# An attention layer and two feed-forward layers on one core: the sums of resident weights go from GpSimd to VectorE, and one block's gate goes to ScalarE

## The chip, the cores and the metric

The kernel runs on one core of a Trainium2 chip, as one program. The time is the device time in microseconds (us), and less is better. A run's time is the median of several executions; the profile is of one execution. The engines are TensorE (PE; its weight loads are PEld), VectorE (DVE), ScalarE (ACT), GpSimd (POOL), and SyncE (SP), which here only issues DMAs.

## The reference

The input is q, k, v of shape (4, 8, 576, 64), a memory matrix and norm for each head, a gate beta, and the weights of two feed-forward layers with 512 model columns and 2048 hidden columns. All is float32.

```
scores = softmax(causal(q k^T / 8));  local = scores v
mem    = (phi(q) M_prev) / (phi(q) z_prev),  phi(x) = max(x,0) + exp(min(x,0))
x      = g * mem + (1 - g) * local, g = sigmoid(beta)     -> 2304 tokens x 512
h1     = x w_in1;  y  = (s * relu(h1)^2 + b) w_out1       first layer
h2     = y w_in2;  out = (h2 * tanh(softplus(h2))) w_out2 second layer
```

## The kernel before, in words

**Precision.** TensorE multiplies float32 matrices as two halves: a high part rounded by a copy (`h`) and a low part, the difference (`l`). Each product is three matmuls: high by high, high by low, low by high. ACT makes the high part of a matrix, DVE the low one (`split`, lines 724 and 725, and the like elsewhere).

**Tokens.** The first layer runs 1024 tokens in four small blocks of 256, then one big block of 512 (`first` and `y_part`, lines 860 and 939). Its last 768 tokens, and all 2304 of the second layer in three times 768, go through a seven-product scheme for 2x2 blocks (`hidden` and `out_product`, lines 1094 and 1167 or 1170). That scheme does not use the weights themselves but sums and differences of their quarters.

**Weights of the first layer.** They are converted early and stay in SBUF, in four parts `r`, as high and low parts (`wih`, `wil`, `woh`, `wol`). For the seven products their sums have to be made from both parts again: 16 tables of nine additions of 128x256 elements each, 144 in all. `resident` (line 787) does this, for the input weights by `IN_TABLE` and for the output weights by `OUT_TABLE`; line 794 is the addition. Four results of each table are stored to DRAM (line 804) and loaded again later, when the seven products want them. All of it is on POOL (`E_SUMS = 'PP'`). The ring `c1` holds the intermediate values in four buffers of 256 columns; they lie in `stage` columns that the first conversion uses before (`conversion_left`). A table takes seven of these buffers, one for each name on its left side, and a stored one comes free when the store has landed.

**Weights of the second layer.** They are converted after the attention has ended (`convert`, lines 687 to 704, and `combine_in`, `combine_out`, whose sums are line 739 and whose splits are line 725). DVE does two steps on each of 32 pieces (lines 701 and 703), and the sums. Two of its work buffers, and the five split buffers `sp`, come to be when the small blocks have left their space (`small_left`).

**The gate of the first layer**, s * relu(h)^2 + b. For a small block, pairs of 256 columns at a time: ACT scales h by s (line 911), DVE multiplies by max(h, 0) (line 917), ACT adds b and rounds to the high part (line 920), DVE makes the low part (line 922). For the big block ACT does it all but the low part: relu (911), square (914), affine (915), high part (919); DVE makes the low part (921). PE's next product into the bank has to wait until the gate has read it.

**The order.** Each operation is a step with an engine, an assumed duration and a key. `Plan.order` simulates all engines ahead of time: whenever an engine is free it takes the ready step with the smallest key, and so it fixes the order of each engine's instructions in the program, SP's too. Engines then run their own instructions strictly in that order. Keys: gates and other elementwise work of the first layer -1 (negative ones first), attention 0 to below 220, first-layer products 500 and up, sums of resident weights and the copies of the weights 499 (`COMBINE`), second conversion 655.2 (`CONV2`), loads and the seven products 990 and up. The plan knows nothing of two engines that slow each other down.

Of the kernel before, what the change touches and what calls it, by code (L numbers as in the profile page):

```python
# [19 lines left out]
P = 128  # L20
# [15 lines left out]
E_SUMS = 'PP'  # L36
# [25 lines left out]
def pool2_us(n):  # L62
    return 0.08 + 0.0028 * n

# [110 lines left out]
class Step:  # L175
    def __init__(self, engine, us, prio, f, waits, bufs, new):
        self.engine, self.us, self.prio, self.f = engine, us, prio, f
        self.waits, self.bufs, self.new = waits, bufs, new
        self.next, self.next_start, self.opens, self.ready = [], [], [], 0.0
        self.lag, self.mode = 0.0, 0  # L180


class Plan:
# [53 lines left out]
    def order(self):  # L237
# [20 lines left out]
        while True:  # L258
            e = 0
            while e < 6:  # L260
# [39 lines left out]
                else:  # L300
                    got.done = end + got.lag
                busy[e] = True
# [43 lines left out]
def attention_then_two_ffn(ctx: ExitStack, tc: tile.TileContext, qk, qz, vm, beta,  # L346
# [108 lines left out]
    def pair(b, p, prio, g, place=None, apart=False):  # L455
# [4 lines left out]
        def add(engine, us, f, r=(), w=(), keep=(), share=1.0):  # L460
            attention_steps.append(plan.add(engine, us, prio, f, r, w, keep=keep, share=share))

# [59 lines left out]
        add(DVE, dve_us(n_e), lambda: nc.vector.scalar_tensor_tensor(ex.t, q_rows(), 0.0, ex.t, op0=ALU.max, op1=ALU.add), [ex, qn_b], [ex])  # L522
        add(DVE, dve_us(n_e), lambda: nc.vector.tensor_tensor(q_rows(), ex.t, z().to_broadcast([P, 2, n_t, D]), op=ALU.mult), [ex, qn_b], [qn_b])
# [149 lines left out]
    def convert(layer, prio, which, r, j, raw, after=()):  # L673
# [10 lines left out]
        def f32():  # L684
# [16 lines left out]
        add(DVE, 0.6, prio, lambda: nc.vector.scalar_tensor_tensor(words()[:, :, 0], words()[:, :, 1], -2 ** 31, words()[:, :, 0],  # L701
                                                                   op0=ALU.bitwise_and, op1=ALU.bitwise_or), [raw, low_words], [signed])
        add(DVE, 0.6, prio, lambda: nc.vector.scalar_tensor_tensor(w.t, w.t, 3, words()[:, :, 0], op0=ALU.logical_shift_left,  # L703
                                                                   op1=ALU.bitwise_or), [raw, signed, w], [w])
# [13 lines left out]
    def split(prio, t, src, r, after=(), done=()):  # L718
# [6 lines left out]
        lo = add(DVE, dve_us(n), prio, lambda: nc.vector.tensor_tensor(t[0](1), src(), t[0](0).bitcast(F32), op=ALU.subtract),  # L725
                 [*r, half], [t[2]], after)
# [8 lines left out]
    def sums(prio, out, table):  # L735
        for f in table:
# [4 lines left out]
            add(DVE, dve_us(256), prio, one, out[1:], out[:1])  # L741
# [45 lines left out]
    def resident(e, prio, hi, lo, names, shape, table, bufs, landed, dest):  # L787
# [4 lines left out]
        def one(o_, x, y, op):  # L792
            def f():
                (nc.vector if e == DVE else nc.gpsimd).tensor_tensor(view(made[o_].t, shape, F32), *(view(made[k].t, shape, F32) if k in made else (hi, lo)[k[0] == "l"](k[1:])
                                                                        for k in (x, y)), op=op)

            steps.append(add(e, dve_us(256) if e == DVE else pool2_us(256), prio, f, [*bufs, *(made[k] for k in {x, y} if k in made)], [made[o_]]))

        for o_, x, y, op in table:
            if o_ not in made:  # L800
                made[o_] = Buf(R["c1"], [P, 256])
            one(o_, x, y, op)
            if o_ in names and (o_, x, y, op) == [row for row in table if row[0] == o_][-1]:
                steps.append(add(DMA, load_us(256), prio, lambda o_=o_: nc.sync.dma_start(dest(names.index(o_)), view(made[o_].t, shape, F32)),
                                 [made[o_]], [landed]))
                steps[-1].lag = 1.5
        return steps

    IN_TABLE = (("A00", "h00", "l00", ALU.add), ("A11", "h11", "l11", ALU.add), ("S1", "h10", "A11", ALU.add), ("S1", "S1", "l10", ALU.add),
                ("S0", "S1", "A00", ALU.subtract), ("S2", "A00", "h10", ALU.subtract), ("S2", "S2", "l10", ALU.subtract),  # L810
                ("A01", "h01", "l01", ALU.add), ("S3", "A01", "S0", ALU.subtract))
# [608 lines left out]
```

## Time and profile before

| | |
|---|---|
| median of three runs | 978.67 us (976.68 to 979.77) |
| the profiled execution | 978.76 us, span 977.0 us |
| PE busy | 944.4 us, 97% |
| PEld busy | 865.5 us, 89% |
| DVE busy | 799.1 us, 82% |
| ACT busy | 666.0 us, 68% |
| POOL busy | 312.5 us, 32% |
| granted TensorE clock, mean | 0.995 |

The span is the time from the first to the last instruction. A busy time is the sum of an engine's instructions with overlaps taken out; matmuls are pipelined, so that a busy PE may still run below its peak. The stages in time: attention with small blocks beside it, and the first conversion, up to about 345 us; small blocks and then the big one, with the second conversion, up to about 505 us; then the seven products of the first layer's rest and of the second layer. In lists of waits, the idle time of an engine before an instruction is put down to what came last of the things the instruction waited for.

### The profile page before, as it was taken

Reading aid. Unit: us, or ns where it says so; the run is one execution under the profiler, and the core shown is the slowest. Engines: PE = TensorE matmul, PEld = TensorE weight load, DVE = VectorE, ACT = ScalarE, POOL = GpSimd, SP = SyncE. Lnnn points to the kernel's source line nnn. Section 1 sums busy time; section 2 is a strip of 40 time slices with the busy share of each in tenths; the row PEclk is TensorE's granted clock in tenths of the full one; section 3 lists DMA queues with packets and bytes.
Section 4 is the critical chain, followed back from the end, with each engine's and each line's share of the span. In section 5 each row is a group of like instructions: output and inputs, shape, how many; then the busy total and the mean of one; then the engine's idle time right before and its main releaser. Section 6 shows DMA issues by size and latency. Waiting matters only on the chain.

```text
span 977.0 us, 19335 instructions
## 1 busy us (share of the span) xinstructions
PE 944.4 (97%) x6599; PEld 865.5 (89%) x6599; DVE 799.1 (82%) x1782; ACT 666.0 (68%) x1433; POOL 312.5 (32%) x495
## 2 busy tenths in 40 slices
PE   5899899999999999998999999999999999999998
PEld 5668688787787899886899999999999999999998
DVE  5999999777767389999887899799966799677874
ACT  4889888877877655668989986467643566344652
POOL 5542566776776756871000000000010000100000
PEclk9999999999999999999999999999999999999999
DMA  9864846999995379899998735896587656676444
GB/s 237 260 192 125 271 143 200 249 273 258 283 268 151 95 215 278 269 301 309 315 336 288 235 124 188 317 335 224 172 297 229 225 173 195 223 235 210 159 144 174
DMA packets 148563, 224.11 MB, mean 229 GB/s; under 512 B 15344, under 2 KB 122864, under 8 KB 141552
## 3 DMA queue, kind: packets, MB, share of 16 engines
q1 hardware_dynamic: 141408, 174.63, 57.9%
q0 software_dynamic: 6624, 48.24, 14.7%
q8 instruction: 52, 0.85, 0.4%
q14 instruction: 47, 0.39, 0.1%
q10 hardware_dynamic: 432, 0.01, 0.0%
HBM read 159.39 MB, written 63.44 MB: 228 GB/s over the span
## 4 chain that ended last, share of the span: by engine, by line
PE 45%; issue 7%; DVE 6%; ACT 6%; DMA 5%; POOL 1%; SPq 0%; POOLq 0%; DVEq 0%; ACTq 0%
PE bank L1094 18%; PE bank L1167 13%; PE bank L1170 6%; PE bank L939 3%; PE bank L860 3%; DMA wo_sums_d<-stage 1%; DVE sc L739 1%; DVE stage L701 1%; DMA woh<-wi_split_d 1%; DMA wi_d<-sc 1%; DVE w32b L703 1%; PE bank L637 1%; DMA woh<-x_d 1%; DVE gl L922 1%; PE bank L615 1%
## 5 line engine op out<-in xcount | busy, mean ns | idle before, releaser
L1094 PE MATMUL bank<-wi,woh 128*128 128x384 f32 x546 | 118.5, 336 | 1.3 <-ACT wol L1112 0.6
L1167 PE MATMUL bank<-wol,S 128*128 128x256 f32 x792 | 107.3, 283 | 0.0
L1167 PEld LDWEIGHTS bank<-wol,S 128*128 128x128 f32 x792 | 101.0, 192 | 0.0
L1094 PEld LDWEIGHTS bank<-wi,woh 128*128 128x128 f32 x546 | 96.2, 188 | 3.2 <-ACT wol L1112 0.9
L1167 PE MATMUL bank<-woh,S 128*128 128x256 f32 x720 | 97.4, 283 | 0.0
L1094 PE MATMUL bank<-wi,wol 128*128 128x384 f32 x414 | 96.1, 335 | 0.0
L1167 PEld LDWEIGHTS bank<-woh,S 128*128 128x128 f32 x720 | 91.4, 192 | 0.0
L574 ACT ACTIVATE Pt<-Pt,mx 128x64 f32<-128x64 f32 (+4 forms) x152 | 83.0, 569 | 3.2 <-DVE mx L566 3.2
L620 ACT COPY PT<-bank 128x384 f32<-128x384 f32 (+2 forms) x160 | 68.8, 492 | 22.8 <-PE bank L615 19.8
L1094 PEld LDWEIGHTS bank<-wi,wol 128*128 128x128 f32 x414 | 73.9, 188 | 0.9 <-DVE woh L1100 0.6
L577 POOL TENSOR_SCALAR Pt<-ex,nm 128x64 f32<-128x64 f32 x152 | 56.9, 396 | 51.0 <-DVE nm L526 38.2
L615 PE MATMUL bank<-ident,Pt 128*128 128x128 f32 x444 | 63.8, 280 | 8.2 <-DVE Pt L592 6.0
L566 DVE CUSTOM_DVE_ANT_0 Pt<-bank,mask 128x64 f32<-128x64 f32 (+3 forms) x152 | 52.0, 373 | 16.1 <-PE bank L556 15.5
L615 PEld LDWEIGHTS bank<-ident,Pt 128*128 128x128 f32 x444 | 51.3, 143 | 12.4 <-POOL ex L520 3.9
L1074 POOL DMA_DIRECT2D woh<-wo_split_d x13 | 6.9, 528 | 164.1 <-DVE g L1100 76.2
L860 PE MATMUL bank<-xh,wi 128*128 128x256 f32 x256 | 42.4, 294 | 5.5 <-DVE rt L917 3.3
L1068 POOL DMA_DIRECT2D woh<-wo_resident_d x4 | 2.4, 590 | 141.0 <-PE bank L1094 105.2
L725 DVE TENSOR_TENSOR woh<-stage,woh 128x1024 fp32r<-128x1024 f32 (+2 forms) x38 | 39.0, 1027 | 9.6 <-ACT woh L724 9.5
L724 ACT CAST woh<-stage 128x1024 fp32r<-128x1024 f32 (+2 forms) x38 | 33.8, 889 | 18.4 <-PE bank L1094 15.6
L724 ACT CAST S<-g 128x384 fp32r<-128x384 f32 x56 | 28.8, 513 | 24.6 <-PE bank L1167 19.2
L917 DVE SCALAR_TENSOR_TENSOR rt<-bank,rt 128x512 f32<-128x512 f32 x32 | 22.0, 686 | 24.8 <-ACT rt L911 24.7
L592 POOL TENSOR_SCALAR Pt<-Pt,rs 128x64 f32<-128x64 f32 (+2 forms) x72 | 38.6, 557 | 10.4 <-DVE rs L595 6.5
(317 smaller groups left out, 2695.5 us busy)
## 6 DMA issues: line engine op xcount, KB each, us to landing
woh<-wo_split_d POOLq DMA_DIRECT2D x13, 1024.0 KB, 5.2
wol<-wo_split_d POOLq DMA_DIRECT2D x11, 1024.0 KB, 5.1
stage<-in_w_in SPq DMA_DIRECT2D x21, 512.0 KB, 5.1
wol<-wi_split_d POOLq DMA_DIRECT2D x10, 1024.0 KB, 5.2
stage<-in_w_out SPq DMA_DIRECT2D x19, 512.0 KB, 5.2
stage<-wi_d SPq DMA_DIRECT2D x24, 384.0 KB, 4.8
stage<-wo_d SPq DMA_DIRECT2D x18, 512.0 KB, 3.5
wo_split_d<-high SPq DMA_DIRECT2D x32, 256.0 KB, 4.7
```

What stands on the lines that cost most here:

```text
L566: nc.vector.tensor_tensor_reduce(at_t(i, t, D + lo, D + hi), x.t[:, a:a + hi - lo], mask[:, SP - w + lo:SP - w + hi], -SCALE, mx.t[:, i, t ...
L574: nc.scalar.activation(at_t(i, t, D, w + D), at_t(i, t, D, w + D), AF.Exp, bias=mx.t[:, i, t + k:t + k + 1], scale=-1.0, accum_out=rs.t[:, ...
L577: add(POOL, 0.33, lambda i=i, t=t: nc.gpsimd.tensor_scalar(at_t(i, t, 0, D), ex.t[:, i, t - lo_t, :], nm.t[:, i, t - lo_t:t - lo_t + 1], 1 ...
L592: (nc.vector if e == DVE else nc.gpsimd).tensor_scalar(x, x, r, *((None, ALU.mult) if e == DVE else (1.0, ALU.mult, ALU.mult)))
L615: nc.tensor.transpose(ps.t[:, x, :], at_t(i, t, c * P, (c + 1) * P), ident)
L620: (nc.vector.tensor_copy if dve else nc.scalar.copy)(PT[i].t[:, x:x + n], ps.t[:, :n])
L724: hi = add(ACT, act_us(n), prio, lambda: nc.scalar.copy(t[0](0), src()), r, [t[2], half], after)
L725: lo = add(DVE, dve_us(n), prio, lambda: nc.vector.tensor_tensor(t[0](1), src(), t[0](0).bitcast(F32), op=ALU.subtract), [*r, half], [t[2] ...
L860: nc.tensor.matmul(ph, w_at(nm, r, cc)[:, o:o + P], x_at(x, cc), start=(begin and part == 0 and cc == 0), stop=(part == 2 and cc == NCC - ...
L1094: nc.tensor.matmul(ps.t[:, :H2], w[i // 4].t[:, j, kk, at_], x[kk].t[:, k], start=begin and part == kk == 0, stop=part == 2 and kk == 1, s ...
L1167: nc.tensor.matmul(acc[t].t[:, :DH], s.t[:, j, t * P:(t + 1) * P], x.t[:, k, q % 4], start=q == part == 0, stop=q == NQ2 - 1 and part == 2)
L1170: nc.tensor.matmul(acc[t].t[:, :H2], x.t[:, k, q % 4, t * P:(t + 1) * P], s.t[:, j], start=q == part == 0, stop=q == NQ2 - 1 and part == 2)
```

## The change

All 144 sums go to DVE (`E_SUMS = 'DD'`). A table now reuses a buffer where an operand is not wanted again and is not itself a result, so that it takes four buffers instead of seven; its additions are chained in the order of the table, and `IN_TABLE` is put in another order. `c1` has a fifth buffer, in the space of the small blocks, which is there from the beginning; for that reason `small_left` now also waits for all sums (`combined`). The assumed lag of a stored sum's landing is 3.0 us instead of 1.5 (`LAND`). The block `j = 3`, the fourth small one, has its gate made as the big block's (`GATED`). Steps with two inputs in SBUF are marked (`two`), and the planner adds 0.35 us (`LOCK`) to a marked step that ends its wait for the engine while a marked step runs on the other of DVE and POOL. The key of the copies of weights gets a name of its own (`KEEP`) and keeps its value.

```diff
-E_SUMS = 'PP'
+E_SUMS = 'DD'
+LOCK = 0.35
+LAND = 3.0
+KEEP = 499.0
+GATED = (3,)
...
+def two(s):
+    s.two = True
+    return s
...
+        beside = [0.0] * 6
...
                 else:
+                    if got.two and beside[DVE + POOL - e] > now:
+                        end += LOCK
                     got.done = end + got.lag
+                    beside[e] = end if got.two else 0.0
...
-        def one(o_, x, y, op):
+        def one(o_, x, y, op, after):
+            o_b, x_b, y_b = (made.get(k) for k in (o_, x, y))
             def f():
...
+            s = two(add(e, 0.05 + dve_us(256) if e == DVE else pool2_us(256), prio, f, [*bufs, *(b for b in (x_b, y_b) if b)], [o_b], after))
+            steps.append(s)
+            return s
+        done = []
         for o_, x, y, op in table:
             if o_ not in made:
-                made[o_] = Buf(R["c1"], [P, 256])
-            one(o_, x, y, op)
+                same = next((k for k in (x, y) if k in made and not any(k in row[1:3] for row in table[table.index((o_, x, y, op)) + 1:]) and k not in names), None)
+                made[o_] = made[same] if same else Buf(R["c1"], [P, 256])
+            done = [one(o_, x, y, op, done)]
...
-                steps[-1].lag = 1.5
+                steps[-1].lag = LAND
...
+    IN_TABLE = (("A11", "h11", "l11", ALU.add), ("S1", "h10", "A11", ALU.add), ("S1", "S1", "l10", ALU.add),
+                ("A00", "h00", "l00", ALU.add), ("S2", "A00", "h10", ALU.subtract), ("S2", "S2", "l10", ALU.subtract),
+                ("S0", "S1", "A00", ALU.subtract), ("A01", "h01", "l01", ALU.add), ("S3", "A01", "S0", ALU.subtract))
...
+        on_act = big or j in GATED
         add(ACT, act_us(m) - 0.04, ew, lambda: nc.scalar.activation(
-            rt.t, ph.t[:, :m], *((AF.Relu,) if big else (AF.Copy, 0.0, sb[:, 0:1]))), [ph], [rt])
-        if big:
+            rt.t, ph.t[:, :m], *((AF.Relu,) if on_act else (AF.Copy, 0.0, sb[:, 0:1]))), [ph], [rt])
+        if on_act:
+            add(ACT, act_us(m), ew, lambda: nc.scalar.activation(rt.t, rt.t, AF.Square), [rt], [rt])
+            add(ACT, act_us(m), ew, lambda: nc.scalar.activation(rt.t, rt.t, AF.Identity, sb[:, 1:2], sb[:, 0:1]), [rt], [rt])
...
-    R["c1"] = Ring("c1").homes(stage, [2048 + 256 * i for i in range(4)], conversion_left)
+    R["c1"] = Ring("c1").homes(stage, [2048 + 256 * i for i in range(4)], conversion_left).more(m1s)
...
-                small_left = add(NONE, 0.0, 0.0, close_small, after=small_steps)
+                small_left = add(NONE, 0.0, 0.0, close_small, after=[*small_steps, combined])
```

The marks stand on the low parts (lines 522 and 523 of the attention, 701, 703, 725, 739, 883, 921 and 922) and on the sums.

## Rows read from the trace of the kernel before

**Rows 1.** Windows by stage: us, each engine's busy us, PE clock, DMA share, GB/s.
```profile
75.00:182.00 107.00, 102.55 (x816) 85.12 (x816) 99.25 (x268) 91.12 (x226) 60.55 (x95) 0.98 0.66 194
182.00:350.00 168.00, 166.84 (x1369) 137.93 (x1369) 110.61 (x361) 126.86 (x343) 120.10 (x216) 1.00 0.78 225
350.00:400.00 50.00, 47.95 (x387) 47.13 (x386) 49.37 (x63) 24.36 (x40) 36.43 (x37) 1.00 0.83 253
400.00:450.00 50.00, 46.22 (x228) 38.65 (x227) 47.58 (x62) 35.16 (x63) 33.35 (x36) 1.00 0.89 278
450.00:525.00 75.00, 74.00 (x359) 64.29 (x358) 63.48 (x133) 69.31 (x137) 0.00 (x0) 1.00 1.00 332
525.00:575.00 50.00, 49.15 (x278) 47.74 (x277) 43.92 (x87) 48.99 (x94) 2.36 (x4) 1.00 0.59 194
```

**Rows 2.** TensorE's timeline: start, us, instructions, [idle before, what ended it].
```profile
364.30 1.22 PE L860 MATMUL bank<-xh,wi 128*128 128x256 f32 x8 [2.05 <-DVE rt L917]
402.29 1.20 PE L860 MATMUL bank<-yh,wi 128*128 128x512 f32 x4 [1.87 <-DVE rt L917]
442.69 1.20 PE L860 MATMUL bank<-yh,wih 128*128 128x512 f32 x4 [1.91 <-ACT g L911]
460.43 1.20 PE L860 MATMUL bank<-yh,wih 128*128 128x512 f32 x4 [0.90 <-ACT g L911]
```

**Rows 3.** ScalarE's timeline, the row ahead of the third wait.
```profile
440.11 0.41 ACT L724 CAST high<-w32b 128x256 fp32r<-128x256 f32 x1 [3.90 <-DVE w32b L703]
```

**Rows 4.** Line L794 in two windows: us, POOL busy us, clock, DMA.
```profile
182.00:350.00 168.00, 55.63 (x72) 1.00 0.78 225
350.00:450.00 100.00, 69.78 (x72) 1.00 0.86 266
```

**Rows 5.** VectorE by line, 350 to 450 us: busy us, mean ns.
```profile
L701 DVE SCALAR_TENSOR_TENSOR stage<-stage 128x512 int32<-128x512 int32 x15 | 15.1, 1008 | 0.0
L922 DVE SCALAR_TENSOR_TENSOR gl<-rt,sb,gh 128x512 fp32r<-128x512 f32 x9 | 10.5, 1172 | 0.3 <-ACT gh L920 0.3
L739 DVE TENSOR_TENSOR sc<-w32b,sc 128x256 f32<-128x256 f32 x12 | 8.0, 668 | 0.1
L917 DVE SCALAR_TENSOR_TENSOR rt<-bank,rt 128x512 f32<-128x512 f32 x9 | 6.1, 682 | 0.8 <-ACT rt L911 0.8
```

**Rows 6.** VectorE by line, 450 to 525 us.
```profile
L701 DVE SCALAR_TENSOR_TENSOR stage<-stage 128x512 int32<-128x512 int32 x7 | 4.8, 689 | 1.5 <-ACT stage L699 1.5
L739 DVE TENSOR_TENSOR sc<-w32b,sc 128x256 f32<-128x256 f32 x6 | 2.5, 422 | 0.1
```

**Rows 7.** VectorE's timeline, one L922 while POOL stands idle.
```profile
344.81 0.75 DVE L922 SCALAR_TENSOR_TENSOR gl<-rt,sb,gh 128x512 fp32r<-128x512 f32 x1 [0.19 <-ACT gh L920]
```

**Rows 8.** Line L794: ns min/median/max, first and last start; what it waited for.
```profile
L794 POOL TENSOR_TENSOR stage<-stage x32: 721/779/1177, 187.6 to 445.6; 128x256 f32<-128x256 f32 x32
...
  DMA wo_sums_d<-stage: 20.4, 14
  DMA wi_sums_d<-stage: 12.8, 4
```

**Rows 9.** VectorE's timeline, two L739 back to back.
```profile
443.62 0.41 DVE L739 TENSOR_TENSOR sc<-w32b,w32b 128x256 f32<-128x256 f32 x1
443.95 0.41 DVE L739 TENSOR_TENSOR sc<-w32b,sc 128x256 f32<-128x256 f32 x1
```

**Rows 10.** VectorE by line, 75 to 182 us.
```profile
L701 DVE SCALAR_TENSOR_TENSOR stage<-stage 128x512 int32<-128x512 int32 x12 | 9.0, 747 | 0.0
```

**Rows 11.** TensorE's waits, 75 to 182 us: total, times, longest.
```profile
PE bank L860 <- DVE rt L917: 1.2, 1, 1.2
```

**Rows 12.** ScalarE by line, whole span: square and affine steps.
```profile
L914 ACT ACTIVATE g<-g 128x512 f32<-128x512 f32 x16 | 10.1, 632 | 0.3
L915 ACT ACTIVATE g<-g,sb 128x512 f32<-128x512 f32 x16 | 13.0, 815 | 0.2
```

**Rows 13.** TensorE's timeline, the last product of the small blocks.
```profile
420.15 0.63 PE L939 MATMUL bank<-gl,woh 128*128 128x256 f32 x4
```

More of the change, by code (lines that the diff above doesn't have):

```diff
@@ L179, in __init__ @@
         self.next, self.next_start, self.opens, self.ready = [], [], [], 0.0
-        self.lag, self.mode = 0.0, 0
+        self.lag, self.mode, self.two = 0.0, 0, False
 class Plan:
@@ L461, in add @@
             attention_steps.append(plan.add(engine, us, prio, f, r, w, keep=keep, share=share))
+            return attention_steps[-1]
         n_t, lo_t, last = len(g), g[0], g[-1]
@@ L700, in convert @@
                                                           TRUNC, 2.0 ** -29 * (1.0 - 2.0 ** -16)), [raw], [low_words])
[L701 to L704, printed above, removed]
+        two(add(DVE, 0.6, prio, lambda: nc.vector.scalar_tensor_tensor(words()[:, :, 0], words()[:, :, 1], -2 ** 31, words()[:, :, 0],
+                                                                       op0=ALU.bitwise_and, op1=ALU.bitwise_or), [raw, low_words], [signed]))
+        two(add(DVE, 0.6, prio, lambda: nc.vector.scalar_tensor_tensor(w.t, w.t, 3, words()[:, :, 0], op0=ALU.logical_shift_left,
+                                                                       op1=ALU.bitwise_or), [raw, signed, w], [w]))
         if layer == 1:
@@ L724, in split @@
         hi = add(ACT, act_us(n), prio, lambda: nc.scalar.copy(t[0](0), src()), r, [t[2], half], after)
-        lo = add(DVE, dve_us(n), prio, lambda: nc.vector.tensor_tensor(t[0](1), src(), t[0](0).bitcast(F32), op=ALU.subtract),
-                 [*r, half], [t[2]], after)
+        lo = two(add(DVE, dve_us(n), prio, lambda: nc.vector.tensor_tensor(t[0](1), src(), t[0](0).bitcast(F32), op=ALU.subtract),
+                     [*r, half], [t[2]], after))
         return hi, lo
@@ L739, in one @@
                 nc.vector.tensor_tensor(o_, x, y, op=op)
-            add(DVE, dve_us(256), prio, one, out[1:], out[:1])
+            two(add(DVE, dve_us(256), prio, one, out[1:], out[:1]))
     def combine_in(prio, r, kk, w0, w1):
@@ L790, in resident @@
         made, steps = {}, []
-        def one(o_, x, y, op):
+        def one(o_, x, y, op, after):
+            o_b, x_b, y_b = (made.get(k) for k in (o_, x, y))
             def f():
-                (nc.vector if e == DVE else nc.gpsimd).tensor_tensor(view(made[o_].t, shape, F32), *(view(made[k].t, shape, F32) if k in made else (hi, lo)[k[0] == "l"](k[1:])
-                                                                        for k in (x, y)), op=op)
-            steps.append(add(e, dve_us(256) if e == DVE else pool2_us(256), prio, f, [*bufs, *(made[k] for k in {x, y} if k in made)], [made[o_]]))
+                (nc.vector if e == DVE else nc.gpsimd).tensor_tensor(
+                    view(o_b.t, shape, F32), *(view(b.t, shape, F32) if b else (hi, lo)[k[0] == "l"](k[1:]) for k, b in ((x, x_b), (y, y_b))), op=op)
+            s = two(add(e, 0.05 + dve_us(256) if e == DVE else pool2_us(256), prio, f, [*bufs, *(b for b in (x_b, y_b) if b)], [o_b], after))
+            steps.append(s)
+            return s
@@ L799, in resident @@
+        done = []
         for o_, x, y, op in table:
             if o_ not in made:
-                made[o_] = Buf(R["c1"], [P, 256])
-            one(o_, x, y, op)
+                same = next((k for k in (x, y) if k in made and not any(k in row[1:3] for row in table[table.index((o_, x, y, op)) + 1:]) and k not in names), None)
+                made[o_] = made[same] if same else Buf(R["c1"], [P, 256])
+            done = [one(o_, x, y, op, done)]
             if o_ in names and (o_, x, y, op) == [row for row in table if row[0] == o_][-1]:
-                steps.append(add(DMA, load_us(256), prio, lambda o_=o_: nc.sync.dma_start(dest(names.index(o_)), view(made[o_].t, shape, F32)),
+                steps.append(add(DMA, load_us(256), prio, lambda o_=o_, b=made[o_]: nc.sync.dma_start(dest(names.index(o_)), view(b.t, shape, F32)),
@@ L1250, in attention_then_two_ffn @@
         for which in ("in", "out"):
-            c1_steps[which][r] += keep_resident(COMBINE, which, r)
+            c1_steps[which][r] += keep_resident(KEEP, which, r)
         for kk in range(2):
```

21 lines of the change are left out of this document (8 added, 13 removed).

## The prediction

> **What bounds the kernel now.** I read the busy time by stage first, then who TensorE waited for, then the timelines around each wait. The stages [rows 1] show TensorE (PE) busy all but 1.16 us of 182 to 350 us, but short by 2.05 us in 350:400, 3.78 in 400:450, 1.00 in 450:525 and 0.85 in 525:575: 7.7 us in all. A busy PE is not PE at its peak, yet the rest of the span is matmuls that the change does not touch, so these few microseconds are what can be won. The long waits stand in [rows 2]: two of 2.05 and 1.87 us ended by VectorE's (DVE) gate L917, then 1.91 and 0.90 us ended by ScalarE's (ACT) L911. In the first two DVE was late: it is busy 49.37 of 50 us in 350:400 [rows 1]. The third is DVE's too, one step back: ACT stood 3.90 us on a split that needed DVE's L703 [rows 3], with the gate queued behind it. So one cause, a full DVE in 350 to 450 us, made 5.83 of the 7.7 us.
>
> DVE is full there partly because of GpSimd (POOL). POOL makes 72 of its 144 sums (L794) in 182:350 and 72 in 350:450, 125.4 us in all [rows 4]; meanwhile DVE's instructions with two SBUF inputs stretch: L701 takes 1008 ns, L922 1172, L739 668 in 350:450 [rows 5], against 689 and 422 ns for L701 and L739 once POOL is quiet [rows 6] and 0.75 us for L922 [rows 7]. L917, with one input in PSUM, stays at 682 ns.
>
> **The change, part by part.**
>
> *Sums leave POOL.* What DVE gets back in 350:450: 15 x (1008 - 689) = 4.8 us on L701's first form, 9 x (1172 - 750) = 3.8 on L922, 12 x (668 - 422) = 3.0 on one form of L739. These are three of some fifteen groups; the others, done alike (L703, the remaining L701 and L739, L725, L883, L921), bring the total to about 32 us of DVE's 97. In 182:350 the same relief is small, about 4 us (L922 and L883), an estimate. POOL also stood 20.4 + 12.8 us on landings of its own stores [rows 8]; that goes too.
>
> *Sums come to DVE.* No row shows a sum of this form on DVE. The nearest is L739, which has the same 128x256 f32 shape: recorded at 422 ns, but issued every 0.33 to 0.34 us back to back [rows 9]. So 144 sums cost 144 x 0.335 = 48 us by the pitch and 144 x 0.422 = 61 us by the record; I take 50, near the pitch, because a record overlaps its successor. They still share time with POOL's attention work: in 75:182 POOL was busy 60.55 us of 107, 57% [rows 1], and L701 took 747 ns [rows 10], 58 above its quiet time. With the sums gone POOL is left with 120.1 - 55.6 = 64.5 us of 168 in 182:350 [rows 1, 4], 38%; 58 x 38/57 x 144 = 5.6 us more. So some 55 us. The bounds are 48 and 61 + 5.6 = 67.
> By the Trainium skill, SBUF — State Buffer, "Who interferes with whom", a two-input Vector instruction and a GpSimd one that reads SBUF exclude each other for the whole instruction. That alone would price each sum at a share of a whole POOL instruction, and the sums here nearer the upper end; the small stretch of L701 [rows 10] says that it rarely falls so.
>
> *Where they land.* The planner gives sums key 499, behind attention (below 220) and the gates (-1), ahead of the second layer's conversion (655.2). So DVE makes them in the holes of attention, from 182 us when the stage columns come free. DVE is busy 110.6 us of 168 there [rows 1]: 57 us of holes plus 4 of relief, for 55 us of sums. Nearly all of them fit, the last by some 350 to 380 us instead of 446 [rows 8]. Five buffers in place allow that: a table now holds four buffers instead of seven. The fifth buffer is free from the start but lets only the first table's first few sums through. The planner's new lock term charges nothing: it delays a step only while the other engine runs a marked one, and with both letters D POOL has no marked step.
>
> *What this costs PE.* DVE would stand at about (110.6 + 55 - 4)/168 = 96% in 182:350. Behind a sum stand the attention's minima, the gates and the low parts, which PE's transposes and products need. Nothing shows PE's loss for this exactly. The nearest row is 75:182, the same mixture with DVE at 99.25 of 107 us [rows 1]: PE waited 1.2 us for the gate [rows 11], so 1.2 x 168/107 = 1.9 us. From above: 400:450, DVE at 95%, with the 1.87 + 1.91 us of [rows 2] traced to DVE, so 3.78 x 168/50 = 12.7 us. From below zero, since first-layer products fill attention's holes on PE. I take 2, as 75:182 is the nearer kind of work. SP's queue carries each store behind its sum, with attention's loads behind it; a late sum holds them, and that is in the same bounds.
>
> *The fourth small block's gate.* Its 8 L917 leave DVE (8 x 0.682 = 5.5 us, [rows 5]). ACT gets 8 squares and 8 affine steps, 8 x (0.632 + 0.815) = 11.6 us [rows 12], less about 2 on cheaper forms of the first and last pass. That lies beside 24.4 us of ACT's 50 in 350:400 [rows 1]; if it ran in 450:525 instead, where ACT has 69.3 of 75, it would cost its length. DVE's two late gates in [rows 2] are this block's, so both waits lose their immediate cause. DVE in 350:450 then holds 97 - 32 - 5.5 = 59 us of 100, plus whatever sums are left over, so the ACT wait of 1.91 us should go too. What is late next is DMA (332 GB/s, share 1.00 in 450:525) and ACT; both bound the second conversion, not PE directly.
>
> *Released later.* The last split buffers now wait for all sums as well as the small blocks. The small blocks' last product starts at 420 us [rows 13]; with the sums done by 380 this costs nothing.
>
> *Sum.* Against the profiled execution, 978.76 us (span 977.0; the median shown, 978.67, is the same to 0.1): -2.05 - 1.87 - 1.91 + 2 = -3.8. Of the other 1.75 us (0.90 in [rows 2] and 0.85 in 525:575) I take 1.0, because the conversion ends earlier and ACT with it (bounds 0 and 1.75): -4.8, **974.0 us**.
>
> **Rivals.**
> 1. *DVE becomes the bound of attention* (slower). If the planned holes are not there on the chip, each sum in front of a minimum or a gate moves PE. At the price of 400:450 that is 12.7 - 6.7 = +6.0, or 984.8 us. It decides once the sums need more than the 61 us of holes, which the upper bound of 67 exceeds. For it: DVE at 96% by my own count. Against: sums have the last key, and 72 of them at most overflow into a stage with 40 us to spare. By the Trainium skill, Perfetto Trace Analysis, "Optimizing Scalar/DVE Operations", a saturated Vector engine is one to take work from, even to GpSimd; the change does the reverse, and by that rule the time would be this rival's. The same section warns that these two engines share a read port, so moving work between them may not help, and the stretched rows here [rows 5, 6] put the warning first.
> 2. *Relief without time* (same). The gates' waits go (3.9), ACT's waits stay or grow because ACT has 10 us more, and attention gives 2 back: 976.9 us. For it: ACT is at 49 of 50 us in 525:575. Against: in 350:450 it idles 40 us.
> 3. *Everything goes* (faster still). All 7.7 us, and the 1.16 us of 182:350 as the plan meets durations it assumed: 969.9 us. For it: the planner's costs know no stretched DVE instruction, so without POOL the order fits better. Against: 93 to 96% of DVE in attention.
> 4. *The sums stay late*: the planner packs attention so that most sums still run after 350 us and the split buffers open late. DVE then has 59 + 50 of 100 us and nothing changes but the engine: 979 us, for the same 350:450 waits. Against: 57 us of holes.
>
> **How the numbers follow.** Chances: the forecast 0.50, rival 1 0.16, rival 2 0.14, rival 3 0.16, rival 4 0.04. A measurement of this kernel tells about 0.3% (2.9 us) from no change, so faster begins below 975.8 and slower above 981.6. The forecast's own range is 971 to 977 (waits in attention 0 to 4), of which 0.42 lies under 975.8 and 0.08 within. With rival 3 that makes 0.58 faster; 0.08 + 0.14 + 0.03 = 0.25 the same; 0.16 and a little of rival 4 make 0.17 slower. The range 967 to 981.5 takes in rivals 2, 3 and 4, with 3 us for what rival 3 may find elsewhere, and leaves out most of rival 1.
>
> **What would show it.** POOL empty of L794, and the sums as DVE rows of about 0.42 us ending before 380 us. L701 at 0.69 us and L922 at 0.75 in 350:450, DVE there near 60 to 75 us of 100. No PE wait on L917 after 350 us; L914 and L915 with 24 instances instead of 16. PE short by under 3 us in 350:575 and by 2 to 4 in 182:350. It is wrong if PE waits on DVE in 182:350 for over 6 us, if the last sum runs after 420 us, or if PE's shortfall in 350:575 stays above 5 us with DVE free.

## The result, and the profile after

The changed kernel takes 970.84 us (median of 4 runs, 969.38 to 971.16) against 979.22 for the kernel before beside it: a ratio of 0.9916 [0.9894, 0.9937], faster by some 8 us. The profiled execution took 969.38 us, its span 967.5. The line numbers moved: L701, L739, L794, L860, L911, L917 and L922 of before are L716, L754, L811, L881, L933, L939 and L944 now, and L703 is L718; where the gate is on ScalarE its low part is L943.

First the busy time by stage, to be held against [rows 1] (columns as there).

```profile
75.00:182.00 107.00, 101.69 (x798) 84.17 (x798) 102.12 (x271) 88.58 (x218) 56.58 (x88) 0.97 0.63 186
182.00:350.00 168.00, 168.00 (x1387) 139.96 (x1387) 140.98 (x462) 129.29 (x348) 77.00 (x151) 1.00 0.84 241
350.00:400.00 50.00, 50.00 (x399) 49.08 (x398) 43.14 (x97) 36.05 (x61) 0.00 (x0) 1.00 0.92 281
400.00:450.00 50.00, 50.00 (x241) 42.04 (x240) 40.49 (x83) 42.74 (x82) 0.00 (x0) 1.00 0.85 282
450.00:525.00 75.00, 74.87 (x376) 67.31 (x375) 61.37 (x126) 67.81 (x130) 0.00 (x0) 1.00 0.95 317
525.00:575.00 50.00, 48.78 (x277) 47.69 (x277) 44.04 (x85) 46.02 (x86) 2.32 (x4) 1.00 0.56 183
```

PE has no hole left from 182 to 450 us, where it was short by 1.16, 2.05 and 3.78 us. POOL is empty after 350. DVE fell from 97 to 84 of 100 us in 350:450 although it now makes sums there, and does 180 instructions instead of 125. What PE still waits for in 350:575, in place of the 6.7 us of [rows 2], is this (us in total, times, longest):

```profile
PE bank L1116 <- ACT wol L1134: 0.7, 1, 0.7
PE bank L1116 <- ACT g L1134: 0.5, 1, 0.5
```

The sums, DVE's busy us by window, against POOL's 55.63 and 69.78 of [rows 4]:

```profile
182.00:350.00 168.00, 40.35 (x97) 1.00 0.84 241
350.00:450.00 100.00, 16.37 (x41) 1.00 0.89 282
```

And DVE's instructions by line in 350 to 450 us, against [rows 5]:

```profile
L716 DVE SCALAR_TENSOR_TENSOR stage<-stage 128x512 int32<-128x512 int32 x14 | 9.6, 689 | 2.8 <-ACT stage L714 2.8
...
L754 DVE TENSOR_TENSOR sc<-w32b,sc 128x256 f32<-128x256 f32 x12 | 5.0, 420 | 0.1
...
L811 DVE TENSOR_TENSOR stage<-woh,wol 128x256 f32<-128x256 f32 x10 | 4.1, 420 | 0.0
...
L944 DVE SCALAR_TENSOR_TENSOR gl<-rt,sb,gh 128x512 fp32r<-128x512 f32 x1 | 0.7, 747 | 0.0
```

L701 went from 1008 to 689 ns, L739 from 668 to 420, L922 from 1172 to 747: the quiet values of [rows 6, 7].

The view that says most in the least space is the chain of work that ended last, cut to 345 to 480 us: shares of that window by engine and line. Before:

```profile
by line: issue 10.1%; PE bank L860 9.2%; DMA wo_sums_d<-stage 8.9%; PE bank L939 8.0%; DVE sc L739 7.0%; DVE stage L701 7.0%; DMA wi_d<-sc 6.1%; DVE w32b L703 5.3%; DMA woh<-x_d 4.8%; DVE gl L922 4.5%; DMA raw<-in_w_in 3.1%; POOL stage L794
```

After:

```profile
by line: PE bank L881 50.6%; PE bank L961 48.9%; PE bank L1116 0.4%; PE bank L957 0.3%
```

Before, the chain ran through DVE's decoding (L701, L703, L739, L922), through the landings of POOL's stores of its sums, and for 17.2% through PE's two lines. After, it is PE alone.

By milestones of the two traces, all of them starts of matmuls: the last attention product starts at 334.2 us instead of 336.4 (-2.2; below, the attention is called over at this point), the first of the seven products at 479.5 instead of 488.0 (-8.5), the outer products (L1170, now L1192) at 549.0 instead of 558.0 (-9.0), and the last product at 963.7 instead of 973.2 (-9.5). So 2.2 us come from the attention, 6.3 from 345 to 480 us, 1.0 from behind it.

### The profile page after: what moved, and what is told of

It reads as the page before. It is cut to its first block, busy times and chain, and to the rows that moved or that the text cites. A ratio compares the mean times of both kernels' runs of the same rounds, so it can differ in the third digit from the quotient of the medians.

```text
span 967.5 us, 19325 instructions
## 1 busy us (share of the span) xinstructions
PE 941.8 (97%) x6599; PEld 865.6 (89%) x6599; DVE 809.2 (84%) x1918; ACT 675.3 (70%) x1449; POOL 195.7 (20%) x351
## 4 chain that ended last, share of the span: by engine, by line
PE 85%; ACT 5%; DVE 4%; DMA 2%; POOL 1%; issue 1%; SPq 0%; POOLq 0%; DVEq 0%; ACTq 0%
PE bank L1116 20%; PE bank L1189 19%; PE bank L881 14%; PE bank L961 13%; PE bank L1192 6%; PE bank L652 5%; PE bank L630 4%; PE bank L571 4%; DMA wil<-in_w_in 1%; DVE Pt L581 1%; DMA wih<-in_qz 1%; ACT Pt L589 1%; POOL stage L710 1%; POOL Pt L592 0%; DVE stage L716 0%
## 5 line engine op out<-in xcount | busy, mean ns | idle before, releaser
L592 POOL TENSOR_SCALAR Pt<-ex,nm 128x64 f32<-128x64 f32 x152 | 60.2, 418 | 75.5 <-DVE nm L541 50.4
L881 PE MATMUL bank<-xh,wi 128*128 128x256 f32 x256 | 43.3, 299 | 4.4 <-ACT xh L903 2.9
L739 ACT CAST woh<-stage 128x1024 fp32r<-128x1024 f32 (+2 forms) x38 | 33.8, 889 | 18.6 <-PE bank L1116 15.6
L607 POOL TENSOR_SCALAR Pt<-Pt,rs 128x64 f32<-128x64 f32 (+2 forms) x72 | 43.0, 617 | 18.5 <-DVE rs L610 7.6
L739 ACT CAST S<-g 128x384 fp32r<-128x384 f32 x56 | 28.8, 514 | 24.6 <-PE bank L1189 19.2
L961 PE MATMUL bank<-gl,woh 128*128 128x256 f32 x256 | 41.8, 288 | 0.0
L881 PEld LDWEIGHTS bank<-xh,wi 128*128 128x128 f32 x256 | 36.0, 199 | 6.1 <-ACT xh L903 3.4
```

What stands on the lines that cost most here:

```text
L592: add(POOL, 0.33, lambda i=i, t=t: nc.gpsimd.tensor_scalar(at_t(i, t, 0, D), ex.t[:, i, t - lo_t, :], nm.t[:, i, t - lo_t:t - lo_t + 1], 1 ...
L881: nc.tensor.matmul(ph, w_at(nm, r, cc)[:, o:o + P], x_at(x, cc), start=(begin and part == 0 and cc == 0), stop=(part == 2 and cc == NCC - ...
L961: nc.tensor.matmul(acc[ec // per].t[:, (ec % per) * n:(ec % per + 1) * n], w_at(nm, fc // FPR, fc % FPR)[:, ec * P:(ec + 1) * P], t(x)[:, ...
```

## The experiments

All times are medians of runs beside the kernel before, whose median was 977.4 to 979.5 us in the five sets (one for the changed kernel, then e1 to e4, e5 to e8, e9 to e11, e12). Where kernels of different sets are compared, I give the difference of the times and that of the ratios, times 978.6 us.

| kernel | us | ratio to before | interval |
|---|---|---|---|
| the changed kernel | 970.84 | 0.9916 | 0.9894 to 0.9937 |
| e9: before, sums on VectorE | 967.18 | 0.9890 | 0.9871 to 0.9910 |
| e1: before, gate on ScalarE | 978.40 | 0.9994 | 0.9982 to 1.0005 |
| e12: both | 968.04 | 0.9886 | 0.9870 to 0.9902 |
| e2: changed, gate back | 976.30 | 0.9976 | 0.9963 to 0.9988 |
| e3: changed, sums back on GpSimd | 983.99 | 1.0053 | 1.0038 to 1.0069 |
| e4: changed, old buffers | 967.34 | 0.9883 | 0.9865 to 0.9900 |
| e7: e4, gate back | 970.65 | 0.9914 | 0.9899 to 0.9930 |
| e8: e4, but in place | 967.34 | 0.9881 | 0.9865 to 0.9898 |
| e10: changed, early sums held | 967.26 | 0.9894 | 0.9869 to 0.9918 |
| e11: e8, third gate moved too | 970.16 | 0.9919 | 0.9902 to 0.9936 |
| e5: changed, idle additions on GpSimd | 1011.55 | 1.0329 | 1.0310 to 1.0349 |
| e6: changed, idle memsets on GpSimd | 969.86 | 0.9902 | 0.9885 to 0.9919 |

My theory at this point was that DVE, slowed by POOL, had held back PE in 350 to 450 us, and that sums and gate each take a part of that away. The rivals were that the gate alone does it, that the sums would be as well on POOL in the new order, and that five buffers in place make it possible.

**The gate alone.**

```diff
+GATED = (3,)
...
+        on_act = big or j in GATED
         add(ACT, ... lambda: nc.scalar.activation(
-            rt.t, ph.t[:, :m], *((AF.Relu,) if big else (AF.Copy, 0.0, sb[:, 0:1]))), [ph], [rt])
-        if big:
+            rt.t, ph.t[:, :m], *((AF.Relu,) if on_act else (AF.Copy, 0.0, sb[:, 0:1]))), [ph], [rt])
+        if on_act:
...
```

> The kernel before with only the fourth small block's gate moved to ScalarE; the sums stay on GpSimd with four buffers. Theory (GpSimd's sums stretch VectorE, and the move of the sums makes most of the gain): VectorE loses 5.5 us of 97 in 350 to 450 us but its L922 and the conversion stay stretched (over 900 ns for the conversion's steps); the two waits of PE on L917 go, ScalarE's stay: 975 to 977.5 us against 979. Rival (the gate was the late thing, the sums matter little): 973 us or less.

Measured 978.40, no gain; neither said so. The stretch stayed, as the theory had it (the conversion's L703, here L704, takes 1000 ns in 345:450, the gate's low part L923 1159). Its waits of PE, 345 to 575 us:

```profile
PE bank L861 <- ACT g L913: 3.5, 2, 3.0
PE bank L861 <- ACT rt L913: 1.3, 1, 1.3
...
PE bank L937 <- DVE xr L974: 0.7, 1, 0.7
```

The two waits on DVE's gate [rows 2] are gone, and 4.8 us stand on ScalarE's step L913 (L911 of before) where 2.81 stood. The gate was where the delay showed, not what made it.

**The changed kernel without the gate's move.**

```diff
-GATED = (3,)
+GATED = ()
```

> The changed kernel without the gate's move: the sums on VectorE in place with five buffers, the fourth small block's gate on VectorE again. Theory: the stretch is gone, VectorE has 84 + 5.5 = 89 of 100 us in 350 to 450 us, PE waits there for under 2.5 us: 971 to 974 us. Rival (the gate made the gain): 975 to 978 us, with PE waiting for the multiply of the gate on VectorE.

Measured 976.30: the rival's time, but not its place. PE is busy all of 345 to 450 us without the move, so no wait on a gate came back. The loss lies behind it, as two windows of this kernel show (columns as in [rows 1]):

```profile
345.00:450.00 105.00, 105.00 (x682) 96.23 (x681) 87.62 (x182) 71.11 (x125) 0.00 (x0) 1.00 0.82 263
450.00:575.00 125.00, 120.35 (x617) 108.59 (x616) 103.74 (x211) 112.58 (x215) 2.31 (x4) 1.00 0.81 268
```

PE's longest waits in the second:

```profile
PE bank L1116 <- ACT woh L1134: 1.2, 1, 1.2
PE bank L1116 <- DVE g L1122: 1.1, 2, 0.6
PE bank L1116 <- ACT g L1134: 1.0, 1, 1.0
```

617 matmuls against 652 in the changed kernel there. These are waits for evacuations of the seven products, with the outer products at 555.5 us instead of 549.0. The plan had found another order for this stage; what in that order makes the waits I did not take apart.

**The sums back on POOL, all else kept.**

```diff
-E_SUMS = 'DD'
+E_SUMS = 'PP'
```

> The changed kernel with the sums back on GpSimd, all else kept: in place, five buffers, the gate on ScalarE, and now with the planner's lock term at work. Theory (which engine adds is what counts): the conversion's steps on VectorE stretch to over 850 ns again wherever sums run beside them; 974 to 977.5 us. Rival (fewer buffers a table and so earlier sums made the gain): 972 us or less, with the last sum before 390 us.

Measured 983.99, slower than before, so both expected times fell. The theory's stretch came (L716 881 ns, L718 983 in 345:450), the rival's early sums did not (the last one starts at 432.1 us). Yet the stretch did not hold PE back there: the lock term has something to charge in this kernel, and in the order that the plan then finds PE is only 0.46 us short in 345:450 though POOL adds there for 65 us. What is lost stands elsewhere: the attention is over at 339.6 us instead of 334.2, and behind 480 us stand longer waits and a stretch at a lower clock (columns of [rows 1]). Whether the stretch costs PE time thus depends on the order too.

```profile
345.00:450.00 105.00, 104.54 (x685) 95.79 (x684) 90.61 (x118) 75.73 (x132) 65.32 (x68) 1.00 0.85 265
450.00:525.00 75.00, 70.81 (x334) 61.83 (x333) 61.62 (x133) 64.84 (x128) 0.00 (x0) 0.95 0.96 322
510.00:520.00 10.00, 6.03 (x21) 5.02 (x20) 8.29 (x18) 6.31 (x13) 0.00 (x0) 0.66 1.00 323
```

**Buffers and order.** One buffer for each name of a table, four of them, and the small blocks' closing without its new wait:

```diff
-                made[o_] = made[same] if same else Buf(R["c1"], [P, 256])
+                made[o_] = Buf(R["c1"], [P, 256])
...
-    R["c1"] = Ring("c1").homes(stage, [...], conversion_left).more(m1s)
+    R["c1"] = Ring("c1").homes(stage, [...], conversion_left)
...
-                small_left = add(..., after=[*small_steps, combined])
+                small_left = add(..., after=small_steps)
```

> The changed kernel with one buffer for each name of a table, four slots, and the split buffers opened without the sums, as before; sums on VectorE and the gate on ScalarE. Theory: the sums end later (seven buffers a table in four slots; the last one after 400 us) but nothing on VectorE is stretched: 971 to 974 us. Rival (five buffers in place are needed for the gain, as VectorE would stand in order behind a landing): 976 us or more.

Measured 967.34: better than the changed kernel by 3.5 us (3.2 by the ratios), though the last sum starts at 421.4 us. Neither the buffers nor early sums are what pays. Nor do sums and stores that come late hold PE back by themselves: here a table takes seven buffers again, as before (last sum at 445.6), and yet PE is busy all of 345 to 450 us. The next has the last two hunks alone, so that the sums are in place in four buffers:

```diff
-    R["c1"] = Ring("c1").homes(stage, [...], conversion_left).more(m1s)
+    R["c1"] = Ring("c1").homes(stage, [...], conversion_left)
...
-                small_left = add(..., after=[*small_steps, combined])
+                small_left = add(..., after=small_steps)
```

> The changed kernel with its sums in place, but four buffers in the stage alone, and without the new wait of the small blocks' closing (the fifth buffer lies in what that closing gives back, so the two go together). It parts what cost the changed kernel some 3 us against the run with the old buffers: the sums in place, or the fifth buffer and its wait. Theory (the fifth buffer's wait and the early sums that it lets into the attention cost it): 966.5 to 968.5, the first sum after 170 us. Rival (a sum in place has to wait for the one before it on the same engine, and that costs): 969.5 to 972, with the last sum before 400 us.

Measured 967.34 again: in place or not is the same, and the theory holds. In the same set the control e6 (below), the changed kernel in all but memsets on POOL, had 969.86. The third kernel keeps the five buffers and their wait, and holds the early sums back:

```diff
-        done = []
+        done = [conversion_left]
```

> The changed kernel with one edit: the first sum of each table also waits until the first layer's conversion has left the stage, so that the fifth buffer stays but no sum runs before that (the changed kernel makes 7 before 182 us). It asks why five buffers cost 3.5 us against four. Theory (the early sums, in the attention, cost it): 966.5 to 968.5, the end of the attention at most 333 us. Rival (the fifth buffer costs it by what it lies in, or by the order that it brings later): 969.5 to 972.

Measured 967.26, 3.6 us under the changed kernel (2.2 by the ratios; the two intervals overlap, the runs themselves lie apart), attention over at 332.0 us: the theory holds. The other traces bear it out: where the early sums run (the changed kernel, e2, e5, e6) the attention is over at 334.2 to 335.7 us, and where they do not (e4, e7 to e10, e12) at 329.9 to 332.2. What the hunk holds back is three sums. DVE's timeline of the changed kernel (start, us):

```profile
105.61 0.66 DVE L811 TENSOR_TENSOR c<-wi 128x256 f32<-128x256 f32 x1
106.30 0.76 DVE L811 TENSOR_TENSOR c<-wi,c 128x256 f32<-128x256 f32 x1
107.10 0.76 DVE L811 TENSOR_TENSOR c<-c,wi 128x256 f32<-128x256 f32 x1
...
179.95 0.46 DVE L811 TENSOR_TENSOR stage<-wi 128x256 f32<-128x256 f32 x1
```

PE's timeline just behind them in the changed kernel:

```profile
111.50 0.80 PE L881 MATMUL bank<-xh,wi 128*128 128x256 f32 x2 [2.17 <-ACT xh L903]
112.99 1.65 PE L881 MATMUL bank<-xh,wi 128*128 128x256 f32 x6 [0.70 <-ACT xh L903]
```

And with the sums held:

```profile
111.43 0.50 PE L881 MATMUL bank<-xh,wi 128*128 128x256 f32 x2 [1.30 <-ACT xh L903]
112.92 0.97 PE L881 MATMUL bank<-xh,wi 128*128 128x256 f32 x6 [0.99 <-ACT xh L903]
```

ScalarE's step L725, which stands ahead of L903, in the changed kernel:

```profile
109.14 0.62 ACT L725 CAST wih<-stage 128x512 fp32r<-128x512 f32 x1 [2.02 <-DVE stage L718]
```

And with the sums held:

```profile
109.07 0.62 ACT L725 CAST wih<-stage 128x512 fp32r<-128x512 f32 x1 [1.11 <-DVE stage L718]
```

The window of 110 to 120 us in the changed kernel, with its mean granted clock, 0.66, as the third figure from the right:

```profile
110.00:120.00 10.00, 7.66 (x38) 7.05 (x39) 9.12 (x23) 8.45 (x20) 4.49 (x6) 0.66 0.93 297
```

And with the sums held, at a clock of 1.00:

```profile
110.00:120.00 10.00, 6.71 (x54) 5.91 (x50) 10.00 (x26) 9.72 (x23) 5.32 (x7) 1.00 1.01 289
```

Three sums, 2.2 us of DVE, where DVE was 102.12 of 107 us busy (101.87 with the sums held). They stand ahead of the conversion's L716 and L718 in DVE's order; ScalarE's L725 waits 2.02 us for that L718 instead of 1.11, x's high part (L903) stands behind it in ScalarE's order, and PE waits 2.17 us for x's high part instead of 1.30. In e6, which runs the same order, PE's wait is 2.17 us too; in the kernel before it is 1.30.

Behind that wait the clock stands at its lower level, 1.2 of 2.4 GHz, for a time: (1 - 0.66) x 10 = 3.4 us of clock lost. Summed so in steps of 10 us up to 960, the changed kernel loses 5.1 us by the clock and this one 3.4. But the clock is not the whole of the early sums' price: the kernel before, e4 and e7 have 0.83 in the same ten microseconds without them, and e4 and e7 lose 5.1 us by the clock as well and have the attention over at 330.6 and 330.8 us. The last product starts 2.0 us sooner with the sums held (961.7 against 963.7). How the 0.9 us of PE's wait becomes the 2 us and more by which the attention ends later is not shown.

**The sums alone.** The kernel before with one word changed:

```diff
-E_SUMS = 'PP'
+E_SUMS = 'DD'
```

> The kernel before with one edit: the sums of resident weights go to VectorE; tables, four buffers and the gate stay as they were. Theory (the time lies in taking the second adder away from VectorE, the rest of the change is worth little): 968 to 972, as the run with old buffers and no gate (970.65), and L701 of the decoding at 0.69 us in 345 to 450. Rival (the sums fill VectorE and only the gate's move makes room, since sums without the gate gave 976.3 with five buffers): 975 to 979.

Measured 967.18, a little below the theory's range and 8 us from the rival's: all of the gain, and 3.7 us more than the whole change (2.5 by the ratios; the two intervals overlap, while the runs themselves, 967.04 to 967.35 and 969.38 to 971.16, lie apart). By stage (columns as in [rows 1]):

```profile
182.00:345.00 163.00, 163.00 (x1345) 135.07 (x1342) 133.35 (x449) 125.92 (x342) 69.45 (x145) 1.00 0.83 240
345.00:450.00 105.00, 105.00 (x672) 95.70 (x671) 92.52 (x197) 71.17 (x127) 0.00 (x0) 1.00 0.87 273
450.00:575.00 125.00, 123.48 (x657) 115.67 (x656) 106.92 (x213) 113.93 (x216) 2.31 (x4) 1.00 0.80 265
```

Its decoding, 345 to 450 us:

```profile
L701 DVE SCALAR_TENSOR_TENSOR stage<-stage 128x512 int32<-128x512 int32 x15 | 10.2, 686 | 4.0 <-ACT stage L699 4.0
```

PE is full from 182 to 450 us with the gate on DVE, whose L917 it never waits for there. By the milestones 6.3 us come from the attention (over at 330.1 us), 5.7 from there to the first of the seven products (476.0), and half a microsecond is lost again behind it. With the gate added:

```diff
-E_SUMS = 'PP'
+E_SUMS = 'DD'
+GATED = (3,)
...
```

> The kernel before with two edits: the sums on VectorE (alone 967.2) and the fourth small block's gate on ScalarE (alone 978.4, no gain). Tables and buffers stay. Theory (with VectorE no longer slowed, the gate is off the path, and what it seemed worth with other buffers, 3.3 to 5.5 us, came with the orders that the plan found there): 966 to 969. Rival (the gate's move is worth something of its own once the sums are off GpSimd): 962 to 965.

Measured 968.04: nothing more (0.9 us worse than e9 by the times, 0.4 better by the ratios). Yet with the old buffers of e4:

```diff
-GATED = (3,)
+GATED = ()
```

> The changed kernel with one buffer for each name of a table, four of them, and without the new wait of the small blocks' closing (as the run that took 967.3), and the fourth small block's gate on VectorE again. It asks what the gate's move is worth where the sums are on VectorE. Theory (the gate is worth the difference that it made with five buffers, 976.3 to 970.8, because the chain of ScalarE and VectorE ahead of each small product is what is left): 971 to 975. Rival (with five buffers the loss without the gate came from the order of the seven products after 500 us, which this order of work does not have): at most 969, and PE's waits in 500 to 575 us under 2 us.

Measured 970.65, just under the theory's range: the gate is worth 3.3 us there (3.0 by the ratios). But the rival's place was the right one: PE is 2.7 us short in 500 to 540 (1.4 in e4), the stage in which e2 lost. And in e8:

```diff
-GATED = (3,)
+GATED = (2, 3)
```

> The kernel with sums in place, four buffers and no new wait of the small blocks' closing (967.34), with the third small block's gate on ScalarE as well as the fourth's. It asks whether more of the same goes on paying. Theory (VectorE no longer sets the small blocks' time where nothing adds on GpSimd, so the third gate only moves work to ScalarE): 967 to 970. Rival (each gate moved is worth what the fourth's was, 3.3 us): 963 to 965.

Measured 970.16, at the theory's upper edge and 2.8 us worse than one gate (967.34; 3.7 by the ratios); the attention is over at 337.0 us instead of 332.2. So the fourth gate's move is worth nothing clear of noise in e1 and e12, 3.3 us in e7 and 5.5 in e2. That is no price of the gate: what it gains in e2 and e7 stands in 500 to 560 us, where the orders differ and no gate of a small block is left. Moving a gate changed the time by up to some 5 us, in both directions.

**Contention by itself.** The order of all other engines' instructions stays as in the changed kernel; POOL gets work on a private buffer that nothing reads, behind the attention:

```diff
+    spare = Buf(R["spare"], [P, 512])
+    add(POOL, 0.8, 656.0, lambda: nc.gpsimd.memset(spare.t, 0.0), [], [spare])
+    for _ in range(100):
+        add(POOL, ..., lambda: nc.gpsimd.tensor_tensor(spare.t[:, :256], spare.t[:, :256], spare.t[:, 256:512], op=ALU.add), [spare])
```

> The changed kernel with 100 additions of two SBUF operands (128x256 f32, on a private buffer that nothing reads) given to GpSimd behind the attention; the instructions of the other engines are the same, in the same order. It asks for the price of a GpSimd that adds beside VectorE, apart from which engine makes the sums. Theory (VectorE's instructions with two SBUF operands are stretched by GpSimd's sums, and this held VectorE back in the kernel before): in 345 to 450 us the mean of the decoding's L716 rises from 0.69 to over 0.95 us and of the sums L754 from 0.42 to over 0.6, GpSimd's additions take over 1.0 us, VectorE's busy time there rises from 87 to over 97 us, PE gets waits of VectorE or ScalarE there, and the time is 974 to 981. Rival (the stretch comes from something else in the kernel before, or VectorE has slack enough for it): L716 under 0.8 us, or the time at most 972.

Measured 1011.55: the theory's mechanism, but 41 us where it gave 3 to 10, and GpSimd's additions under the 1.0 us that it gave them. The window of 345 to 450 us:

```profile
345.00:450.00 105.00, 77.22 (x503) 71.74 (x503) 98.48 (x115) 45.03 (x74) 82.65 (x94) 0.85 0.52 161
```

Lines of POOL and DVE in it:

```profile
L1286 POOL TENSOR_TENSOR spare<-spare 128x256 f32<-128x256 f32 x94 | 83.3, 887 | 7.4
...
L811 DVE TENSOR_TENSOR stage<-woh,wol 128x256 f32<-128x256 f32 x12 | 10.8, 905 | 0.0
...
L716 DVE SCALAR_TENSOR_TENSOR stage<-stage 128x512 int32<-128x512 int32 x9 | 8.9, 990 | 0.4 <-ACT stage L714 0.4
...
L943 DVE TENSOR_TENSOR gl<-rt,gh 128x512 fp32r<-128x512 f32 x8 | 8.6, 1081 | 0.1
```

PE's main wait there:

```profile
PE bank L881 <- ACT rt L933: 23.8, 6, 8.1
```

L716 went from 689 to 990 ns, a sum from 420 to 905. DVE is 98.48 of 105 us busy and does 115 instructions instead of 184, as stretched as in [rows 5], and with the sums to make besides. ScalarE waits 35.6 us for DVE's L943 ahead of its L933, so comes late for PE's banks, and the clock falls to a mean of 0.85: 22.1 us of clock lost in the run against 5.1, so at most 17 of the 41 us are the clock's, an upper bound because PE was also idle in that time. The control replaces the additions by

```diff
+    for _ in range(150):
+        add(POOL, ..., lambda: nc.gpsimd.memset(spare.t, 0.0), [spare])
```

> The control to it: the same private buffer and the same place, but 150 memsets of 128x512 on GpSimd, which read nothing from SBUF. Theory (it is GpSimd's reading of SBUF operands that slows VectorE): L716 stays at most 0.75 us and L754 at most 0.46 in 345 to 450 us, and the time is 969.5 to 972.5, that of the changed kernel. Rival (any busy GpSimd slows VectorE): L716 over 0.85 us, and the time over 973.

Measured 969.86. The same window:

```profile
345.00:450.00 105.00, 105.00 (x682) 96.23 (x681) 86.59 (x183) 82.55 (x145) 72.73 (x138) 1.00 0.87 280
```

The same lines:

```profile
L1286 POOL MEMSET spare<- 128x512 f32 x138 | 72.7, 527 | 7.9
...
L716 DVE SCALAR_TENSOR_TENSOR stage<-stage 128x512 int32<-128x512 int32 x15 | 10.3, 687 | 2.2 <-ACT stage L714 2.2
```

PE waits for nothing there. POOL is 72.73 us busy and DVE shows no stretch: 687 ns. It is POOL's reading from SBUF that counts, not its being busy. The Trainium skill, SBUF — State Buffer, "Who interferes with whom", says just that: a two-input Vector instruction collides with a GpSimd one that reads SBUF, not with one that only writes. The runs agree, with 990 and 687 ns.

## Why the prediction was right, and where not

974.0 was forecast, 969.38 came in the profiled execution, 970.84 in the median: inside the range, just under the likeliest case's own 971 to 977, and by the terms nearest to rival 3 (969.9). The range, 967 to 981.5, took in four mechanisms, so lying inside it says little.

- **The waits of 350 to 450 us, -5.83.** Right in size: 6.3 us came from 345 to 480, which also holds the 0.90 us wait. The cause, a DVE that POOL's sums make full, was right too; what was wrong is the share of the gate's move. I gave 3.92 us to it, since these were the gate's waits; e1 takes the gate away and gains nothing, e9 takes the sums away and gains all of it. The relief of DVE was well sized: each of DVE's groups of [rows 5] and its like, at its number of instructions in the kernel before and its length in the changed one, gives 32 us, as I had. DVE's busy time fell by less, from 96.95 to 83.63 us, because 41 sums ran there and because, with the sums left out, it did 139 instructions there instead of 125 in spite of the gate's eight fewer.
- **The step that failed: "+2" for new waits in attention.** It came out as -2.2, which is 4.2 of the 4.6 us between forecast and profiled execution. I expected DVE at 96% in 182:350 and took its price from 75:182, the nearest crowded row. DVE came to 140.98 of 168, 84%, mainly because 41 of the sums ran after 350 us and 7 before 182: those in between take 37 us of DVE, not 55. DVE's other work there is some 7 us shorter than before, where I had put 4. PE has no wait there. Also wrong was that PE's 7.7 us are all that can be won: e9, with no early sums, has the attention over at 330.1 instead of 336.4 us. The clock is not the bulk of these 6.3 us, as e4 and e7 have 330.6 and 330.8 with the same 5.1 us of clock lost as the kernel before. They came with the sums' leaving POOL. Whether DVE's relief does that, or POOL's own steps that no longer queue behind sums, no run separates.
- **The other 1.75 us, -1.0.** Right in size, by luck: the 0.90 us went, but it lies before 480 us and is in the 6.3. The 0.85 us of 525:575 did not go (PE is short by 1.22 us there now), and the 1.0 us behind 480 came in halves, before and behind the start of the outer products.
- **The price of a sum on DVE.** I took the pitch, 0.335, and 50 us for 144, some 55 with POOL's share. The records of the 144 add up to 60.4 us, but most of them overlap the instruction before; what each adds behind the end of that one comes to 54.3 us, 0.38 each. The pitch was the right price.
- **The fifth buffer and in-place sums, priced at nothing.** That only the first table's first sums get through was right: three. But they, 2.2 us on DVE in the stage where [rows 1] have it at 99.25 of 107, cost 2 to 3.6 us (e10). The last sum ran at 387.4, not by 380, and that it did mattered to nobody (e4: 421.4).
- **The signs.** POOL without L794, 420 ns sums, L716 at 0.69 and L944 at 0.75, no wait on the gate after 350, 24 instances of the square (16 and 8) and PE short by 1.4 us in 350:575: as said. PE short by nothing in 182:350, not by 2 to 4. DVE in 350:450 at 84 of 100 us, not 60 to 75, because of the 41 sums left and of work that came forward.
- **The rivals.** Rival 1 had the right kind of danger and the wrong stage: PE waits for nothing in 182:350, and sums ahead of other work on DVE cost something in 75:182 only. By the Trainium skill, Perfetto Trace Analysis, "Optimizing Scalar/DVE Operations", unloading a saturated Vector engine, even on to GpSimd, may make sense. Here loading it, and emptying GpSimd, is what paid (967.18), so the same section's warning about the shared port decided. Rival 2 fell, as ACT's waits did not stay. Rival 3, with a chance of 0.16, came nearest: of the 8.84 us that PE was short in 182:575, 1.35 are left. Rival 4 fell with over 100 of 144 sums done by 350 us.

That the lock term charges nothing in the changed kernel was an argument from the code and no run shows its price; e3 is the only run in which it acts.

## What to carry to other kernels

When two engines slow each other, the price of moving work from one to the other is not its duration on the new one: take off what its absence gives back, which was some 32 us of VectorE in 350:450 alone here, and look whether the waits that it causes carry another instruction's name. Try the one constant that carries the mechanism by itself before shipping it with companions; here it gave 967.2, and its companions gave some 3 us of that back. And where a planner orders everything anew, an edit's price moves by some 3 to 5 us with the order, so only edits that leave the order alone, as the idle additions do, price a mechanism. How much of the gain of 11 us in e9 is the stretch, and how much the new order that comes with it, is not shown: e5 shows that the stretch alone can hold PE back, e3 that an order can hide most of it in 345:450.

## What the runs showed of the hardware

The stretch is large and lies mostly on VectorE's side. Beside back-to-back GpSimd additions (e5, 345 to 434 us, which leaves out the time after the last of them) these two lines read:

```profile
L718 DVE SCALAR_TENSOR_TENSOR w32b<-w32b,stage 128x512 int32<-128x512 int32 x6 | 7.3, 1218 | 0.0
...
L754 DVE TENSOR_TENSOR sc<-w32b,sc 128x256 f32<-128x256 f32 x4 | 3.8, 953 | 0.0
```

In the changed kernel they take 690 and 420 ns (350 to 450 us). Both grew by the same 0.53 us, though one is much longer than the other: here the stretch was an addition to each instruction and not a factor, so a short instruction lost most for its length. The means of 990 and 905 ns above mix stretched instructions with some that were not. GpSimd's own addition took 887 ns in the mean, against 739 at its shortest. GpSimd seems to pay as well: in 182 to 345 us most of its one-operand steps were longer once the sums were on VectorE (350 and 397 ns below; one form was shorter, 1021 and 979), and POOL kept 77.0 us in 182:350 where I had expected 64.5. By line, before:

```profile
L577 POOL TENSOR_SCALAR Pt<-ex,nm 128x64 f32<-128x64 f32 x80 | 26.1, 350 | 26.9 <-DVE nm L526 18.7 <-PE bank L615 5.5 <-DVE nm L518 2.6
```

After:

```profile
L592 POOL TENSOR_SCALAR Pt<-ex,nm 128x64 f32<-128x64 f32 x84 | 31.5, 397 | 48.8 <-DVE nm L541 29.7 <-PE bank L630 17.4 <-PE bank L571 0.9
```
